# An attention-and-mixing kernel: a searched order for every engine, paired score blocks, longer rows for q and k, weights in halves

## The chip, the cores and the metric

One core of a Trainium2 chip. The metric is device time in microseconds (us) of a whole execution, and lower is better. Fast executions of one kernel differ by up to about 1% (the kernel before: 191.07 to 193.41 us in one set of rounds), so every ratio here is between fast runs made in the same rounds on the same chip. Three runs of the kernel before are slow and left out: 287.37 us (TensorE's granted clock at 0.557), 193.45 and 193.88 us.

In the profile PE is TensorE's matmuls, PEld its weight loads, DVE VectorE, ACT ScalarE, POOL GpSimd and SP the engine that starts transfers. "The span" is the profiled execution without its launch; the time lies about 2 us over it.

## The reference, cut to what matters

```python
def _attn_ref(q, k, v, n_sink, window):          # q, k, v: 4 batches, 8 heads, 768 positions, 64
    scores = scale * np.matmul(q, k.transpose(0, 1, 3, 2))
    keep = is_sink | in_window                    # the first 4 positions, and the last 128
    scores = np.where(keep, scores, -1e9)
    a = softmax(scores)                           # (cut)
    return np.matmul(a, v)

def _moe_ref(x, mu_k, mu_r, w_k, w_v, w_r):       # x: 4 x 768 x 512, the attention's result
    x_prev = ...                                  # x, one position later (cut)
    xk = mu_k * x + (1.0 - mu_k) * x_prev
    xr = mu_r * x + (1.0 - mu_r) * x_prev
    k = np.maximum(xk @ w_k, 0.0)                 # the "hidden layer", 512 -> 1024
    v = k * k @ w_v                               # its "product", 1024 -> 512
    r = 1.0 / (1.0 + np.exp(-(xr @ w_r)))         # the "gate"
    return r * v
```

Of the kernel before, what the change touches and what calls it, by code (L numbers as in the profile page):

```python
# [18 lines left out]


class Plan:

# [8 lines left out]
    def __init__(self):  # L31
        self.ops, self.pools, self.buf = [], {}, {}

# [3 lines left out]
    def op(self, engine, cost, emit, rank, reads=(), writes=(), take=(), hold=(), port=False,  # L37
           lag=None, service=0.0):
        self.ops.append(dict(engine=engine, cost=cost, emit=emit, rank=rank, reads=list(reads),
                             writes=list(writes), take=list(take), hold=list(hold), port=port,  # L40
                             lag=90.0 if lag is None else lag, service=service))

    def schedule(self):
# [21 lines left out]
        owner = {key: pool for o in ops for pool, key in o["take"]}  # L65
        free = {name: [(0.0, j) for j in range(len(t))] for name, t in self.pools.items()}
# [8 lines left out]
        ready = {}  # L75
        for i, o in enumerate(ops):
            at[i] = 0.0
            if not left[i]:
                ready.setdefault(o["engine"], set()).add(i)
        clock, port, dma = {}, {}, 0.0  # L80
# [3 lines left out]
        while len(order) < len(ops):  # L84
            best = None
            for engine, some in ready.items():
                now = clock.get(engine, 0.0)
                pick = None
                for i in some:
                    o = ops[i]  # L90
                    t = max(now, at[i])
                    if o["port"]:
                        t = max(t, port.get("DVE" if engine == "POOL" else "POOL", 0.0))
                    ok = True
                    for name, _ in o["take"]:
                        if not free[name]:
                            ok = False
                            break
                        t = max(t, min(free[name])[0])
                    if not ok:  # L100
                        continue
                    if pick is None or (t, o["rank"], i) < (pick[0], ops[pick[1]]["rank"], pick[1]):
                        pick = (t, i)
                if pick is None:
                    continue
                t0 = pick[0]
                if best is None or t0 < best[0]:
                    best = (t0, pick[1])
# [3 lines left out]
            ready[o["engine"]].discard(i)  # L112
            for name, key in o["take"]:
                b = min(free[name])
                free[name].remove(b)
                where[key] = b[1]
                self.buf[key] = self.pools[name][b[1]]
            clock[o["engine"]] = t + o["cost"]
# [3 lines left out]
            if o["service"]:  # L122
                dma = max(dma, t + o["cost"] + 1300.0) + o["service"]
                end = dma + 600.0
            o["start"], o["end"] = t, end
            order.append(i)
# [5 lines left out]
            for j, whole in then[i]:  # L132
# [8 lines left out]
                if not left[j]:  # L141
                    ready.setdefault(ops[j]["engine"], set()).add(j)
        return order

    def run(self):
        for i in self.schedule():
            self.ops[i]["emit"]()
# [3 lines left out]
def kernel(  # L151
# [34 lines left out]
    pool("sc", 1, [128, 2, 512], FP32, psum)  # L186
    pool("bank", 6, [128, 512], FP32, psum)
    for name in ("ks", "qs", "vs"):
        pool(name, 3, [128, 2, H, D], FP32)
# [39 lines left out]
    def load(u, names, rank, h0=0, h1=H):  # L229
        b, T = divmod(u, NT)  # L230
        for name in names:
            src = {"k": k, "q": q, "v": v}[name]
            for g in range(2):
                s0 = 256 * T + 128 * g

                def emit(key=(name, u), src=src, g=g, s0=s0):
                    nc.sync.dma_start(  # L237
                        out=buf[key][:, g, h0:h1, :],
                        in_=src[b, h0:h1, s0:s0 + 128, :].rearrange("h p d -> p h d"))
                rows = 128 * (h1 - h0)  # L240
                first = g == 0 and h0 == 0
                P.op("SP", rows * 0.9 + 60.0, emit, rank, service=rows * 1.19 + 60.0,
                     take=[(name + "s", (name, u))] if first else (),
                     hold=() if first else [(name, u)],
                     writes=[(name, u, g, hp) for hp in range(h0 // 4, (h1 + 3) // 4)])

    def load_weight(dst, src, key, service, rank):
        P.op("SP", 1000.0, lambda: nc.sync.dma_start(
            out=dst, in_=src.rearrange("(c p) f -> p c f", p=128)), rank, service=service,
            writes=[key])  # L250

    load(0, "kq", -100, 0, 4)
    load(0, "kq", -99, 4, 8)
    load(0, "v", -98)
    load_weight(wk32, moe_w_k, "wk32", 4900.0, -97)
    load(1, "kq", -96)
    load_weight(wr32, moe_w_r, "wr32", 2600.0, -95)
    load(1, "v", -94)
    load_weight(wv32, moe_w_v, "wv32", 5200.0, -93)
    for u in range(2, U):  # L260
        load(u, "kqv", -92 if u == 2 else 10 * u - 18)
# [6 lines left out]
    def const_op(engine, cost, emit, writes=(), reads=(), rank=-50):  # L268
# [3 lines left out]
    const_op("DVE", 300.0, lambda: nc.vector.memset(warm, 0.0), ["warm"])  # L272
    ident32 = tile1([128, 128], FP32, "ident32")
    ident = tile1([128, 128], BF16, "ident")
    const_op("POOL", 500.0, lambda: make_identity(nc, ident32), ["ident32"], rank=-60)
    const_op("POOL", 240.0, lambda: nc.gpsimd.tensor_copy(out=ident, in_=ident32), ["ident"],
             ["ident32"])

    mask = tile1([128, 2, 2, 2, 128], BF16, "mask")
    mask0 = tile1([128, 2, 3, 128], BF16, "mask0")  # L280

    def keep(ap, kind):
        if kind == "U":
            nc.gpsimd.affine_select(out=ap, in_=ap, compare_op=ALU.is_ge, fill=0.0, base=-1,
                                    pattern=[[0, 2], [-1, 128]], channel_multiplier=1)
        else:
            nc.gpsimd.affine_select(out=ap, in_=ap, compare_op=ALU.is_ge, fill=0.0, base=0,
                                    pattern=[[0, 2], [1, 128]], channel_multiplier=-1)

    def make_mask0():  # L290
        nc.gpsimd.memset(mask0, 1.0)
        keep(mask0[:, :, 0, :], "D")
        keep(mask0[:, :, 1, :], "U")
        keep(mask0[:, :, 2, :], "D")
        nc.gpsimd.memset(mask0[0:NS, :, 0:2, :], 1.0)

    def make_mask():
        nc.gpsimd.memset(mask, 1.0)
        for a in range(2):
            keep(mask[:, a, :, 0, :], "U")  # L300
            keep(mask[:, a, :, 1, :], "D")

    const_op("POOL", 2300.0, make_mask0, ["mask0"], rank=-55)

    def make_ones():
        for t in P.pools["vb"]:
            nc.gpsimd.memset(t[:, :, :, D:D + 1], 1.0)

    const_op("POOL", 400.0, make_ones, ["ones"], rank=-54)

    xts = [tile1([128, NC, S + 2], BF16, f"xt{i}") for i in range(2)]

    def make_edges():
        for t in xts:
            nc.gpsimd.memset(t[:, :, 0:2], 0.0)

    const_op("POOL", 200.0, make_edges, ["edges"], rank=-45)
# [3 lines left out]
    hmask = tile1([32, H, D + 1], BF16, "hmask")  # L321

    spread = tile1([128, 128], BF16, "spread")

    def make_spread():
        nc.gpsimd.memset(spread, 0.0)
# [3 lines left out]
    def make_hmask():  # L330
        nc.gpsimd.memset(hmask, 1.0)
        nc.gpsimd.affine_select(out=hmask, in_=hmask, compare_op=ALU.is_ge, fill=0.0, base=0,
                                pattern=[[-4, H], [0, D + 1]], channel_multiplier=1)
        nc.gpsimd.affine_select(out=hmask, in_=hmask, compare_op=ALU.is_ge, fill=0.0, base=3,
                                pattern=[[4, H], [0, D + 1]], channel_multiplier=-1)

    def make_sinks():
        for t in ksink + vsink:
            nc.gpsimd.memset(t, 0.0)
        for t in vsink:  # L340
            nc.gpsimd.tensor_copy(out=t[0:32, :, D:D + 1], in_=hmask[:, :, D:D + 1])

    const_op("POOL", 800.0, make_spread, ["spread"], ["ident"], rank=-44)
    const_op("POOL", 2000.0, make_hmask, ["hmask"], rank=-43)
    const_op("POOL", 2400.0, make_sinks, ["sinks"], ["hmask"], rank=-42)
    const_op("POOL", 2700.0, make_mask, ["mask"], rank=-41)


    wk_sb = tile1([128, NC, Dff], BF16, "wk_sb")
    wr_sb = tile1([128, NC, Dm], BF16, "wr_sb")  # L350
    wv_h = tile1([128, NF, Dm], BF16, "wv_h")
    for i in range(4):
        sl = slice(256 * i, 256 * i + 256)
        P.op("DVE", dve(1024, 0.52), lambda sl=sl: nc.vector.tensor_copy(
            out=wk_sb[:, :, sl], in_=wk32[:, :, sl]), 2 + i, reads=["wk32"], writes=[("wk", i)],
            port=True)
    for i in range(2):
        P.op("DVE", dve(1024, 0.52), lambda i=i: nc.vector.tensor_copy(
# [353 lines left out]
```

## The kernel before: the parts that the change touches

The work is cut into 12 units, each of 256 positions of one batch. The kernel's text lists operations with what they read, write and take from pools of buffers; a planner then puts all of them in one order. It is a greedy planner: at each step it takes the engine that can start soonest, and on it the operation that can start soonest by a small timing model. The order on each engine is then fixed: on the chip an engine never skips an operation whose input is late.

```python
while len(order) < len(ops):
    best = None
    for engine, some in ready.items():
        ...                                       # (cut) earliest start t of each ready operation
                    if pick is None or (t, o["rank"], i) < (pick[0], ops[pick[1]]["rank"], pick[1]):
                        pick = (t, i)
```

Scores use one buffer of two banks of the accumulator memory (PSUM), everything else of TensorE's results the other six banks. The block of scores of one head pair is one operation; it has 64 rows of contraction, and two heads run side by side in the two halves of the array:

```python
pool("sc", 1, [128, 2, 512], FP32, psum)
pool("bank", 6, [128, 512], FP32, psum)
...
for (lhs, o0, o1, rhs) in jobs:
    for a in range(2):
        rows = slice(64 * a, 64 * a + 64)
        nc.tensor.matmul(out=sc[:, a, o0:o1], lhsT=lhs[rows], rhs=rhs[rows], start=True, stop=True)
```

q, k and v are loaded one position and head at a time, 256 bytes each, and each weight in one transfer:

```python
nc.sync.dma_start(out=buf[key][:, g, h0:h1, :],
                  in_=src[b, h0:h1, s0:s0 + 128, :].rearrange("h p d -> p h d"))
...
load_weight(wk32, moe_w_k, "wk32", 4900.0, -97)
```

Eight warm-up matmuls with an operand of zeros run before the first transpose. The masks are stored once per head, and v is cast to 16 bits on GpSimd.

The softmax here doesn't subtract the row's maximum and nothing guards it: scores larger than these inputs give would overflow.

## Time and profile before

| | before |
|---|---|
| time, median of the runs first given (lowest to highest) | 192.47 us (192.15 to 193.44) |
| span of the profiled run (its time) | 189.7 us (191.44) |
| last matmul ends | 186.0 us |
| TensorE streaming in all, from start-to-start distances | 147.9 us |
| of it done by 35.0 us | 12.0 us |
| streaming after 35 us / time that it takes to the last matmul | 135.9 / 151.0 us |

"Streaming" is what the matmuls need when they follow each other without a gap. It has to be worked out from distances between starts, because the busy time in the profile counts the overlap of neighbours twice. The lines that carry this table are in the prediction below; one of the waits from 35 us on is added here. The columns are engine and line, what the wait was for, us in all, times, the longest.

```profile
PEld L476 <- issue: 8.5, 27, 0.7
```

L476 is the score block, and "issue" says that the trace shows no event for which its weight loads waited: this is the time in which TensorE goes into the 64-row form.

### The profile page before, as it was taken

What the parts mean: (1) busy time and instruction counts of PE and PEld (TensorE: products, weight loads), DVE (VectorE), ACT (ScalarE), POOL (GpSimd) and SP (SyncE); (2) the same over time, 40 slices, a digit from 0 to 9 for tenths busy, and PEclk for the clock granted to TensorE, in tenths of its full rate; (3) what the DMA queues carried; (4) which work ended last, traced back from release to release, by engine and by line L of the source; (5) the groups of instructions that cost most, each with busy time, mean ns of one, the idle gap of its engine ahead of it and who ended that gap; (6) DMA issues with size and microseconds to landing.
All of it is one profiled execution on the core that took longest, in us unless ns stands there. A gap on an engine that the chain in (4) does not pass through costs nothing.

```text
span 189.7 us, 4373 instructions
## 1 busy us (share of the span) xinstructions
PE 171.4 (90%) x1676; PEld 111.1 (59%) x1676; DVE 155.9 (82%) x375; ACT 133.4 (70%) x225; POOL 31.9 (17%) x65
## 2 busy tenths in 40 slices
PE   7245699989999999999999999999799999999992
PEld 2123466548647758658549468478368577575740
DVE  0538986999999999989999969989989888888512
ACT  0762767669987978959939859949749679575240
POOL 8990030030420310001501002003400000000000
PEclk9955559999999999999999999999999999999999
DMA  6999989999999999999899891030021030020302
GB/s 109 225 387 252 297 212 358 205 206 225 216 213 276 225 194 252 233 254 235 190 233 278 183 273 59 0 111 3 0 75 41 0 114 0 3 111 0 116 0 111
DMA packets 81573, 30.70 MB, mean 162 GB/s; under 512 B 76432, under 2 KB 76432, under 8 KB 81552
## 3 DMA queue, kind: packets, MB, share of 16 engines
q1 hardware_dynamic: 80496, 30.42, 68.0%
q8 instruction: 13, 0.21, 0.5%
q10 hardware_dynamic: 1056, 0.00, 0.3%
q14 instruction: 8, 0.07, 0.1%
HBM read 24.12 MB, written 6.29 MB: 160 GB/s over the span
## 4 chain that ended last, share of the span: by engine, by line
PE 64%; DVE 20%; DMA 5%; ACT 4%; SPq 4%; issue 2%; ACTq 0%; DVEq 0%
PE bank L598 18%; PE bank L636 18%; PE bank L621 8%; PE sc L476 6%; DMA ks<-in_k_dram 5%; PE bank L517 4%; DVE xk L577 4%; PE bank L395 4%; SPq L237 3%; DVE kk L611 3%; DVE e L493 3%; DVE xr L577 2%; DVE qb L382 2%; PE bank L449 2%; PE bank L556 2%
## 5 line engine op out<-in xcount | busy, mean ns | idle before, releaser
L484 ACT ACTIVATE e<-sc 128x1024 bf16<-128x1024 f32 (+1 forms) x48 | 46.8, 974 | 26.4 <-PE sc L476 26.0
L598 PE MATMUL bank<-xk,wk_sb 128*128 128x256 bf16 x384 | 54.7, 279 | 0.1
L636 PE MATMUL bank<-wv_h,kk 128*128 128x512 bf16 x192 | 47.1, 380 | 0.0
L598 PEld LDWEIGHTS <-wk_sb 128*128 128x128 bf16 x384 | 35.2, 100 | 7.0 <-issue 1.1
L493 DVE TENSOR_TENSOR e<-e,mask 128x1024 bf16<-128x1024 bf16 (+1 forms) x48 | 31.1, 653 | 8.5 <-ACT e L484 8.4
L607 ACT ACTIVATE rl<-bank 128x512 bf16<-128x512 f32 x48 | 29.2, 630 | 7.4 <-PE bank L598 6.6
L413 POOL CAST vb<-vs 128x512 bf16<-128x512 f32 x24 | 17.4, 741 | 74.4 <-DMA vs<-in_v_dram 45.7
L636 PEld LDWEIGHTS <-kk 128*128 128x128 bf16 x192 | 17.1, 98 | 19.1 <-issue 1.1
L621 PE MATMUL bank<-wr_sb,xr 128*128 128x512 bf16 x96 | 24.5, 380 | 0.0
L577 DVE SCALAR_TENSOR_TENSOR xk<-td,mu,xt 128x256 bf16<-128x256 bf16 x48 | 23.2, 507 | 0.5
L611 DVE TENSOR_TENSOR kk<-rl 128x512 bf16<-128x512 bf16 x48 | 21.0, 450 | 2.7 <-ACT rl L607 2.6
L476 PE MATMUL sc<-qt,kt 64*128 64x128 bf16 (+1 forms) x256 | 19.1, 250 | 4.4 <-ACT qt L406 2.6
L577 DVE SCALAR_TENSOR_TENSOR xr<-td,mu,xt 128x256 bf16<-128x256 bf16 x48 | 22.4, 490 | 0.0
L645 DVE SCALAR_TENSOR_TENSOR ob<-th,bank 128x512 f32<-128x512 f32 x24 | 16.3, 681 | 6.7 <-PE bank L636 6.7
L517 PE MATMUL bank<-vb,e 128*128 128x65 bf16 x352 | 20.1, 197 | 1.6 <-DVE e L493 1.5
L517 PEld LDWEIGHTS <-e 128*128 128x128 bf16 x352 | 17.1, 100 | 5.6 <-DVE e L493 2.9
L533 DVE TENSOR_TENSOR x<-bank,rec 128x256 bf16<-128x256 f32 x48 | 19.6, 419 | 0.7
L476 PEld LDWEIGHTS <-kt 64*128 64x128 bf16 x256 | 9.5, 96 | 15.5 <-issue 13.9
L382 ACT CAST kb<-ks 128x512 bf16<-128x512 f32 x24 | 14.9, 667 | 4.6 <-DMA ks<-in_k_dram 4.6
L382 DVE CAST qb<-qs 128x512 bf16<-128x512 f32 x24 | 13.2, 563 | 5.0 <-DMA qs<-in_q_dram 5.0
L406 ACT COPY qt<-bank 128x512 bf16<-128x512 bf16 x24 | 14.9, 622 | 2.9 <-PE bank L395 2.9
L627 ACT ACTIVATE th<-bank 128x512 f32<-128x512 f32 x24 | 15.8, 657 | 1.0 <-PE bank L621 1.0
(49 smaller groups left out, 171.2 us busy)
## 6 DMA issues: line engine op xcount, KB each, us to landing
vs<-in_v_dram SPq DMA_DIRECT2D x24, 256.0 KB, 4.8
out_dram<-ob SPq DMA_DIRECT2D x24, 256.0 KB, 2.2
ks<-in_k_dram SPq DMA_DIRECT2D x22, 256.0 KB, 5.4
qs<-in_q_dram SPq DMA_DIRECT2D x22, 256.0 KB, 5.1
wk<-in_moe_w_k_dram SPq DMA_DIRECT2D x1, 2048.0 KB, 9.3
wv<-in_moe_w_v_dram SPq DMA_DIRECT2D x1, 2048.0 KB, 13.8
wr<-in_moe_w_r_dram SPq DMA_DIRECT2D x1, 1024.0 KB, 7.9
ks<-in_k_dram SPq DMA_DIRECT2D x4, 128.0 KB, 3.4
```

The costliest lines, as they stand in the source:

```text
L382: P.op(by, cost, lambda copy=copy, raw=raw, rk=rk, hs=hs: copy(out=buf[rk][:, :, hs, :], in_=buf[raw][:, :, hs, :]), rank + half, port=by ...
L476: nc.tensor.matmul(out=sc[:, a, o0:o1], lhsT=lhs[rows], rhs=rhs[rows], start=True, stop=True)
L484: nc.scalar.activation(out=buf[ek][:, :, lo:], in_=buf[sck][:, :, lo:], func=AF.Exp, scale=scale)
L493: nc.vector.tensor_tensor(out=buf[ek][:, :, lo:], in0=buf[ek][:, :, lo:], in1=m, op=ALU.mult)
L517: nc.tensor.matmul(out=o[:, g, a, :], lhsT=e[:, a, e0:e0 + 128], rhs=rhs, start=(T == 0 and i == 0), stop=(i == len(blocks) - 1), skip_gro ...
L533: P.op("DVE", dve(256), lambda ok=ok, rk=rk, c=c: nc.vector.tensor_tensor(out=buf["x", u][:, :, 128 * c:128 * c + 128].rearrange("p g (a d ...
L577: nc.vector.scalar_tensor_tensor(out=buf[key][:, c0 + i, :], in0=buf[tk][:, i, :], scalar=mu[w][:, c0 + i:c0 + i + 1], in1=xt[:, c0 + i, t ...
L598: nc.tensor.matmul(out=ps[:, i, :], lhsT=wk_sb[:, c, 128 * f:128 * f + 128], rhs=xk[:, c, :], start=(c == 0), stop=(c == NC - 1), skip_gro ...
L607: P.op("ACT", act(512), lambda psk=psk, rk=rk: nc.scalar.activation(out=buf[rk], in_=buf[psk].rearrange("p (i t) -> p i t", i=2), func=AF. ...
L611: P.op("DVE", dve(512, 0.52), lambda f2=f2, rk=rk: nc.vector.tensor_tensor(out=buf["kk", u][:, 2 * f2:2 * f2 + 2, :], in0=buf[rk], in1=buf ...
L621: nc.tensor.matmul(out=buf[psk], lhsT=buf["xr", u][:, c, 128 * g:128 * g + 128], rhs=wr_sb[:, c, :], start=(c == 0), stop=(c == NC - 1))
L636: nc.tensor.matmul(out=buf[psk], rhs=wv_h[:, f, :], lhsT=buf["kk", u][:, f, 128 * g:128 * g + 128], start=(f == 0), stop=(f == NF - 1))
```

## The change

Its intent is to shorten the loading start and to remove TensorE's gaps after it. Five things change together:

1. The greedy choice is replaced by a fixed list for each engine, found beforehand by swapping operations in the timing model.
2. Score blocks of two head pairs run one after the other as one operation, with two score buffers (four banks), which leaves four banks for all else.
3. q and k are loaded with two neighbouring positions per row, 512 bytes. The transposed copies then hold even and odd positions apart, and ScalarE writes them with a stride when it empties the bank.
4. w_k and w_v come in halves, and loads of other units go between them.
5. Filling matmuls on zeros are put into TensorE's gaps before 45 us of the model, to keep its clock up; set-up work moves from GpSimd to VectorE, and so does the first cast of v.

```diff
+ORDER = {
+    "PE": (
+        77, 80, 93, 83, 86, 104, 96, 119, 101, 107, 125, 129, 122, 112, 116, 145, 136, 91, 171,
...                                              (cut: 324 + 379 + 226 + 32 + 79 places)
-        while len(order) < len(ops):
+        lines = {engine: list(line) for engine, line in ORDER.items()}
+        while any(lines.values()):
...
+                while t - now > 300.0 and now < self.fill_until:
...                                              (cut: takes a free bank)
+                    now += 225.0
+                    order.append(("fill", self.pools["bank"][b[1]]))
...
-    pool("sc", 1, [128, 2, 512], FP32, psum)
-    pool("bank", 6, [128, 512], FP32, psum)
+    pool("sc", TOGETHER, [128, 2, 512], FP32, psum)             # TOGETHER = 2
+    pool("bank", 8 - 2 * TOGETHER, [128, 512], FP32, psum)
...
+                out=buf[key][:, h0:h1, :, :].rearrange("p h j d -> p h (j d)"),
+                in_=src[b, h0:h1, 256 * T:256 * T + 256, :].rearrange(
+                    "h (p j) d -> p h (j d)", j=2)), rank,
...
+LOADS = ("kq0", "v0", "kq1", "wka", "v1", "wkb", "wr", "wva", "wvb")
...
+                    out=buf[key][:, 2 * half:2 * half + 2, :, :].rearrange(
+                        "p c g (t j) -> p c j (g t)", j=2),
...
+                     emit=lambda cs=cs: [scores(i) for i in cs], rank=r, lag=PE_LAG,
+                     take=[("sc", ("sc", u, i)) for i in cs],
```

## The prediction

> **What bounds the kernel now.** I read the page first, then stretches of 5 us, the timeline of TensorE, the counts of matmuls up to the time at which the weights are in, and the waits.
>
> ```profile
> span 189.7 us, 4373 instructions
> PE 171.4 (90%) x1676; PEld 111.1 (59%) x1676; DVE 155.9 (82%) x375; ACT 133.4 (70%) x225; POOL 31.9 (17%) x65
> ...
> PEclk9955559999999999999999999999999999999999
> ...
> PE 64%; DVE 20%; DMA 5%; ACT 4%; SPq 4%; issue 2%; ACTq 0%; DVEq 0%
> ```
>
> TensorE carries most of the chain that ends last, with VectorE next. TensorE's clock is at half in slices 2 to 5.
>
> ```profile
> 5.00:10.00 5.00, 1.56 (x16) 1.04 (x17) 2.81 (x2) 3.66 (x7) 4.86 (x10) 0.88 1.29 230
> 10.00:15.00 5.00, 2.46 (x18) 1.17 (x18) 1.95 (x3) 3.23 (x5) 3.81 (x9) 0.50 1.00 395
> 15.00:20.00 5.00, 2.26 (x32) 1.91 (x31) 4.53 (x12) 1.59 (x4) 0.00 (x0) 0.50 1.27 216
> 20.00:25.00 5.00, 3.65 (x31) 2.64 (x30) 3.89 (x12) 3.65 (x6) 0.00 (x0) 0.50 1.08 301
> 25.00:30.00 5.00, 5.00 (x34) 3.10 (x32) 5.00 (x9) 3.14 (x5) 1.67 (x2) 0.57 0.85 271
> ```
>
> The columns are the stretch, its length, busy time of PE, PEld, DVE, ACT and POOL, the granted clock, the DMA share and GB/s. Until 25 us TensorE is mostly idle, and what it does runs at half clock, while the DMA is full: 395 GB/s when a weight flows, 216 to 230 GB/s when rows of q, k and v of 256 bytes do. So the start is bound by loading, and made worse by the clock.
>
> Busy time overstates the rest, as matmuls overlap. I take the distance from start to start instead:
>
> ```profile
> 111.45 0.28 PE L517 MATMUL bank<-vb,e 128*128 128x65 bf16 x4
> 111.67 0.40 PE L476 MATMUL sc<-qt,kt 64*128 64x256 bf16 x6
> 112.00 0.61 PE L598 MATMUL bank<-xk,wk_sb 128*128 128x256 bf16 x4
> 112.44 0.39 PE L395 MATMUL bank<-ident,kb 128*128 128x128 bf16 x4
> ```
>
> Four 256-column matmuls take 112.44 - 112.00 = 0.44 us, 0.109 each. In the same way 512 columns take 0.216, 128 take 0.056, 65 take 0.029 and 130 take 0.058. With the page's counts: hidden layer 384 x 0.109 = 41.9, its product 192 x 0.216 = 41.5, gate 96 x 0.216 = 20.7, transposes 288 x 0.056 = 16.1, values 352 x 0.029 + 64 x 0.058 = 13.9, sinks 32 x 0.109 = 3.5, spread 0.9, scores about 9.4 if the two 64-row halves run together. That is 147.9 us of streaming; the span has 42 us more. Where are they?
>
> ```profile
> L598 PE MATMUL bank<-xk,wk_sb 128*128 128x256 bf16 x32 | 6.4, 349 | 0.0
> ...
> L476 PE MATMUL sc<-qt,kt 64*128 64x256 bf16 x16 | 2.9, 356 | 3.7 <-ACT qt L406 1.9 <-ACT e L484 1.8
> L517 PE MATMUL bank<-vb,e 128*128 128x65 bf16 x46 | 2.8, 220 | 0.0
> ...
> L621 PE MATMUL bank<-wr_sb,xr 128*128 128x512 bf16 x8 | 2.1, 379 | 0.0
> ```
>
> These are the groups of the first 34.5 us (the last weight is cast from 34.2 on). Weighted as above, all groups in that stretch make 11.3 us of streaming. So 23 us are lost in the first 34.5. From there to the last matmul's end near 186.0, 136.6 us of streaming take 151.5: 15 lost. The tail is 3.7 (last VectorE operation at 186.1, then the store).
>
> ```profile
> ACT e L484 <- PE sc L476: 26.0, 27, 2.1
> ...
> PEld L476 <- issue: 13.9, 37, 1.1
> ```
>
> The second line is the score blocks. In the timeline above the values before them need 4 x 0.029 and end at 111.57; the next full-row matmul starts at 112.00. The block takes 0.43 where three concurrent pairs of 256, 128 and 128 columns need 0.21, so entering and leaving the 64-row form costs about 0.21 us. I count 46 such groups in the instruction order, about 37 after 34.5 us: 7.9 of the 15 us lost. The other 7 are waits, mostly for VectorE:
>
> ```profile
> 132.38 0.48 DVE L577 SCALAR_TENSOR_TENSOR xr<-td,mu,xt 128x256 bf16<-128x256 bf16 x1
> 132.78 1.58 DVE L577 SCALAR_TENSOR_TENSOR xk<-td,mu,xt 128x256 bf16<-128x256 bf16 x2
> ```
>
> Two operations that take 0.40 each from start to start take 1.50 while GpSimd casts v (it is busy 3.73 us between 130 and 135). TensorE then waits over 1 us for a masked score block at 135.
>
> **What the Trainium skill says.**
> "TensorE: Matmul & The Clock Gate", Part 1, has warm matmuls at N/2.4 GHz + 2.5 ns (55.6 and 215.7 ns) and a clock at half after about 3.4 us of idleness. The trace agrees: 56 and 216 ns, and 0.50 after the eight warm-up matmuls ended at 4.9 us.
> "TensorEngine Tiling (Array Packing)", Key Properties, says that a change of tiling mode drains TensorE. The 0.21 us per block agrees.
> "DMA: Bandwidth & Descriptors", Specifications, gives 512 B as the least transfer for line rate. The trace has only one side of it: 256 B at about 216 GB/s, weight rows of 2 to 4 KB at 395.
> "SBUF — State Buffer", two separate sides, says that VectorE and GpSimd lock a port pair against each other. The stretched xk agrees.
>
> **The change part by part.**
> *Scores of two pairs together.* Two score buffers (4 PSUM banks instead of 2), the other pool shrinks from 6 banks to 4. Groups fall from 46 to 24. About 18 of them come after the start: 37 - 18 = 19 fewer x 0.21 = 4.0 us, on the path, since TensorE is the bound there. ScalarE can also do two exponentials without the wait of 26.0 us in the list.
>
> *q and k in rows of 512 bytes.* Per-row estimate from the two rates above: 256 B at 216 GB/s is 1.19 ns, 4096 B at 395 is 10.4 ns, a straight line gives 1.8 ns for 512 B, 285 GB/s. q and k of one unit (256 positions of one batch) are 1.05 MB: 3.7 us instead of 4.9. In return the transposed copies on ScalarE write with a stride; it is busy 70%, so even 0.15 us x 48 hides.
>
> *Order of loads, weights in halves.* With these rates, and the first k at about 4.0 us (4.5 before, less bytes), I add up in the new order: q and k of unit 0 whole at 8, v at 11, k of unit 1 at 13, the first half of w_k at 15.5, q of unit 2 at 18.6, the second half at 21, w_v's first half at 27, w_r at 29.5, the rest of w_v at 34. So the hidden layer of unit 0 can start at about 17 (before: 23.7, at half clock). The last weight is no earlier than before, but more loads of other units have gone ahead of it.
>
> *Filling matmuls.* The eight warm-ups become 42, all ahead of or between the pieces of unit 0's attention: 19 before the first transpose. They should hold the clock at 1.0. Cold ones take 0.43 us, so 19 may end near 7 to 8 us and delay the first transpose by up to 1 us; that is hidden, as w_k is not there before 15.5.
>
> *Sum to 35 us.* In the new order of TensorE I count 12.2 us of streaming ahead of the first product (needs w_v's first half, cast at 27.6), 14.0 ahead of the gate (w_r cast at 31), and 17.6 ahead of the first product that needs the second half of w_v. From 31 on: 17.6 - 14.0 = 3.7 and some switches, so about 35.0 for 17.6 us of work. Before had 11.3 at 34.5: the start gives about 6 us.
>
> *The rest.* 147.9 - 17.6 = 130.3 of streaming, 18 x 0.21 = 3.8 of switches, and other waits, 7 before. The searched order should remove some, four banks may add some: I take 5. That gives 139.1: the last matmul at 174.1, with the tail of 3.7 a span of 177.8. The measured time lies 1.7 to 2.8 us over the span (191.44 in the profiled run and 192.47 median against 189.7), so about 180.
>
> *Moved to VectorE.* Memsets before data comes (hidden) and the cast of the first v, 2 x 0.34. The masks shrink and repeat by a stride of zero; same sizes computed, no change.
>
> **The rivals.**
> *VectorE becomes the bound.* From start to start one unit with a full window needs q casts 2 x 0.335, masks 4 x 0.60, reciprocals and x 4 x 0.43, differences 2 x 0.34, mixes 8 x 0.395, squares 4 x 0.335, outputs 2 x 0.60: 11.2 us, plus up to 1.3 of GpSimd's lock. TensorE needs 12.8 + 0.4. With both over 90% full, every slip of a fixed order shows. For it: VectorE is at 4.9 to 5.0 of 5 us between 40 and 70. Then the waits go to 12 us: time 187.
> *Four banks starve TensorE.* A unit takes 19 banks; in 13.2 us each of four may be held 2.8 us (before, with six, 4.1). Fills of 0.45 to 1.7 us plus 0.6 of evacuation fit, unless an evacuation is late. Worth 0 to 5 us.
> *The start is not better*, because the clock falls anyway where the filling matmuls stop, or 512-byte rows are no faster: the 6 us shrink to 2, time 184.
> *The order beats my guess*: waits of 1 us, time 176.
>
> **Range and chances.** Rivals two to four move the 180 by -4 to +5, and the first by +7. They would hardly all come together, since a slow start leaves slack for VectorE. I put 179.5, 8 in 10 within 174 to 186. Within 2% means over 188.6: it needs the start's gain and the switches' both lost.
>
> **What would show it.** Clock 1.0 from 10 us to the end; DMA near 285 GB/s while q and k flow; the first hidden-layer matmul at 16 to 18 us; 24 score groups, with two blocks in about 0.64 us; the wait of the weight loads of scores down to about half of 13.9; the last matmul near 174. I am wrong if the clock falls again, if TensorE has more than 10 us of waits for banks or for VectorE after 35 us, or if the hidden layer starts after 20 us.

## The result, and the profile after

The changed kernel takes 183.54 us (median of 4 runs, 183.11 to 184.3), the kernel before 192.46 in the same rounds (192.15 to 193.44). The ratio is 0.9532, with a 95% interval of 0.9486 to 0.9579. Ratios here are the mean time of one kernel's fast runs over that of the other's fast runs of the same rounds, so they are not quite the ratio of the medians. The verdict is faster, inside the predicted range and 4.0 us over the predicted time.

From the page, the span, the busy times, the clock and the chain that ended last:

```profile
span 181.3 us, 4366 instructions
...
PE 169.3 (93%) x1687; PEld 114.2 (63%) x1710; DVE 152.9 (84%) x389; ACT 139.0 (77%) x225; POOL 23.2 (13%) x47
...
PEclk9999759999999999999999999999999999999999
...
PE 73%; DVE 19%; ACT 4%; issue 2%; DVEq 0%
```

TensorE now carries 73% of the chain (before 64%), and no transfer is in it any more. The clock falls later and for a shorter time than before, but it does fall. (1710 weight loads and 1687 matmuls: 23 matmul records are missing, each of which looks like a gap of up to 0.22 us in the timeline.)

The stretches from 15 us on, with the same columns as in the prediction:

```profile
15.00:20.00 5.00, 2.81 (x45) 1.98 (x43) 3.13 (x10) 4.07 (x8) 0.61 (x1) 1.00 1.13 310
20.00:25.00 5.00, 3.47 (x27) 2.04 (x29) 4.24 (x12) 3.33 (x5) 0.71 (x1) 0.50 1.07 285
25.00:30.00 5.00, 4.91 (x58) 3.99 (x59) 4.89 (x11) 4.16 (x8) 0.48 (x1) 0.82 1.01 355
30.00:35.00 5.00, 4.25 (x64) 3.30 (x61) 4.94 (x14) 4.12 (x9) 0.00 (x0) 1.00 1.10 354
```

Loading is faster between 15 and 20 us (310 GB/s in place of 216), yet TensorE has little more to do than before. And from 25 us on VectorE, the third busy column, is full (TensorE's busy time, the first, counts overlap twice). The timeline of unit 0 says why (start, length, engine, line, what; in brackets the idle time before and what ended it):

```profile
4.01 0.62 ACT L507 CAST kb<-ks 128x512 bf16<-128x512 f32 x1 [1.41 <-DMA ks<-in_k_dram]
5.82 0.43 DVE L507 CAST qb<-qs 128x512 bf16<-128x512 f32 x1 [1.91 <-DMA qs<-in_q_dram]
7.86 0.39 PE L519 MATMUL bank<-ident,kb 128*128 128x128 bf16 x4
...
18.01 0.59 ACT L704 COPY xt<-bank 128x512 bf16<-128x512 bf16 x1 [0.46 <-PE bank L698]
...
19.20 0.66 DVE L484 CAST wk_sb<-wk 128x1024 bf16<-128x1024 f32 x1
20.11 0.68 DVE L484 CAST wk_sb<-wk 128x1024 bf16<-128x1024 f32 x1
21.05 0.42 DVE L709 TENSOR_TENSOR td<-xt 128x512 bf16<-128x512 bf16 x1
...
24.92 0.83 DVE L719 SCALAR_TENSOR_TENSOR xk<-td,mu,xt 128x256 bf16<-128x256 bf16 x1
26.30 1.29 PE L740 MATMUL bank<-xk,wk_sb 128*128 128x256 bf16 x8
33.25 0.68 DVE L482 TENSOR_SCALAR wv_h<-wv 128x1024 bf16<-128x1024 f32 x1
35.33 1.03 PE L778 MATMUL bank<-wv_h,kk 128*128 128x512 bf16 x4
```

The first half of w_k landed at 16.9 us, but the first hidden-layer matmul runs at 26.30, later than before (23.7). It waits for xk, the last piece of which VectorE finishes at 24.92 + 0.83 = 25.75. VectorE could have started the difference for it when the copy of x ended at 18.60; in its order the casts of w_k and pieces of other work come first, and it starts at 21.05. That is the first half of x. The last xk needs the second half, which is copied only at 22.69, and then two casts of q and one xr stand before and between the pieces of xk. TensorE puts four transposes ahead of the hidden layer after that. In the same way the first half of w_v landed at 28.5 and is cast only from 33.25 to 35.2; the first product follows at 35.33. The prediction had counted 12.2 us of streaming ahead of this product and put it at 27.6: the work ahead of it was right, and it came 7.7 us later.

The trace of before shows the same wait. There w_k had landed at 16.2 us (6.92 + 9.3), and the hidden layer started at 23.74, when xk was ready.

Counting the matmuls of the first 35.0 us and giving each its start-to-start distance, the changed kernel has 12.2 us of streaming done (hidden layer 32 x 0.109, values 56 x 0.029, their sinks 8 x 0.058, scores 20 x 0.109 / 2 and 32 x 0.056 / 2, transposes 64 x 0.056, sinks 8 x 0.109, spread 0.2), the kernel before 12.0 in the same way (it has fewer transposes, and eight gate matmuls). So the whole expected head start shrinks to 0.2 us.

Then the score blocks, in TensorE's timeline at the place that the prediction showed of before:

```profile
112.47 1.04 PE L740 MATMUL bank<-xk,wk_sb 128*128 128x256 bf16 x8
113.44 0.61 PE L602 MATMUL sc<-qt,kt 64*128 64x256 bf16 x12
113.98 0.40 PE L698 MATMUL bank<-ident,x 128*128 128x128 bf16 x4
```

Eight hidden-layer matmuls take 8 x 0.109 and end their streaming at 113.34. The next full-row matmul starts at 113.98: 0.64 us for two blocks that need 2 x 0.22 (0.109 + 2 x 0.056 each), so one switch costs 0.20 for two blocks, where at the place shown of before it was 0.21 for each. Taking this difference at every switch after 35 us that no wait interrupts gives 0.200 to 0.211 us for 38 of the 40 before and 0.201 to 0.205 for 18 of the 19 after, in the middle 0.202 both times. The corresponding wait from 35 us on:

```profile
PEld L602 <- issue: 1.3, 6, 0.3
```

The 8.5 us of before have become 1.3. Here is the whole account, with a switch taken as 0.202 us:

| | before | after | gain |
|---|---|---|---|
| streaming done by 35.0 us | 12.0 | 12.2 | 0.2 |
| last matmul ends | 186.0 | 177.6 | |
| time from 35 us to there | 151.0 | 142.6 | |
| streaming in that time | 135.9 | 135.7 | (the 0.2 above) |
| lost in that time | 15.1 | 6.9 | |
| of it switches | 40 x 0.202 = 8.08 | 19 x 0.202 = 3.84 | 4.24 |
| other waits | 7.02 | 3.06 | 3.96 |
| tail after the last matmul | 3.7 | 3.7 | 0 |

0.2 + 4.24 + 3.96 = 8.4 us, which is 189.7 - 181.3. The third experiment measures the price of a switch in another way. (The total of 147.9 us is the prediction's. From the same distances the scores need 9.7 us, not 9.4, which takes 0.3 us from the other waits on both sides and leaves the gain.)

Loading, from the page's line of packets:

```profile
DMA packets 57124, 30.69 MB, mean 169 GB/s; under 512 B 26896, under 2 KB 51472, under 8 KB 57104
```

Before, 76432 of 81573 packets were under 512 B; now 26896 of 57124 are, and 24576 of these are rows of v.

### The profile page after: what moved, and what is told of

The parts are those of the page before. It is cut to its first block, busy times and chain, and to the rows that moved or that the text cites. A ratio compares the mean times of both kernels' runs of the same rounds, so it can differ in the third digit from the quotient of the medians.

```text
span 181.3 us, 4366 instructions
## 1 busy us (share of the span) xinstructions
PE 169.3 (93%) x1687; PEld 114.2 (63%) x1710; DVE 152.9 (84%) x389; ACT 139.0 (77%) x225; POOL 23.2 (13%) x47
## 2 busy tenths in 40 slices
DMA packets 57124, 30.69 MB, mean 169 GB/s; under 512 B 26896, under 2 KB 51472, under 8 KB 57104
## 4 chain that ended last, share of the span: by engine, by line
PE 73%; DVE 19%; ACT 4%; issue 2%; DVEq 0%
PE bank L778 20%; PE bank L740 18%; PE bank L763 10%; PE sc L602 6%; PE bank L798 5%; PE bank L659 5%; PE bank L519 5%; DVE xk L719 3%; PE bank L698 3%; DVE xr L719 3%; DVE e L636 2%; DVE x L675 2%; PE bank L647 2%; DVE kk L753 2%; ACT e L622 2%
## 5 line engine op out<-in xcount | busy, mean ns | idle before, releaser
L740 PE MATMUL bank<-xk,wk_sb 128*128 128x256 bf16 x384 | 51.9, 274 | 0.7 <-ACT th L769 0.4
L622 ACT ACTIVATE e<-sc 128x1024 bf16<-128x1024 f32 (+1 forms) x48 | 44.8, 963 | 1.0 <-PE sc L602 0.9
L749 ACT ACTIVATE rl<-bank 128x512 bf16<-128x512 f32 x48 | 27.9, 608 | 13.5 <-PE bank L740 6.5
L763 PE MATMUL bank<-wr_sb,xr 128*128 128x512 bf16 x87 | 23.7, 379 | 0.5
L719 DVE SCALAR_TENSOR_TENSOR xr<-td,mu,xt 128x256 bf16<-128x256 bf16 x48 | 23.3, 497 | 0.1
L527 ACT COPY qt<-bank 128x512 bf16<-128x512 bf16 x24 | 17.9, 744 | 7.0 <-PE bank L519 6.9
L753 DVE TENSOR_TENSOR kk<-rl 128x512 bf16<-128x512 bf16 x48 | 19.8, 425 | 1.5 <-ACT rl L749 1.5
L527 ACT COPY kt<-bank 128x512 bf16<-128x512 bf16 x24 | 17.8, 743 | 2.6 <-PE bank L519 2.6
L704 ACT COPY xt<-bank 128x512 bf16<-128x512 bf16 x24 | 14.1, 587 | 6.4 <-PE bank L698 6.2
L769 ACT ACTIVATE th<-bank 128x512 f32<-128x512 f32 x24 | 14.1, 606 | 4.0 <-PE bank L763 4.0
L602 PE MATMUL sc<-qt,kt 64*128 64x128 bf16 (+1 forms) x256 | 14.7, 248 | 0.9 <-ACT kt L527 0.8
```

The source lines that it names most:

```text
L527: nc.scalar.copy(out=buf[key][:, 2 * half:2 * half + 2, :, :].rearrange("p c g (t j) -> p c j (g t)", j=2), in_=buf[psk].bitcast(BF16)[:, ...
L622: nc.scalar.activation(out=buf[ek][:, :, lo:], in_=buf[sck][:, :, lo:], func=AF.Exp, scale=scale)
L719: nc.vector.scalar_tensor_tensor(out=buf[key][:, c0 + i, :], in0=buf[tk][:, i, :], scalar=mu[w][:, c0 + i:c0 + i + 1], in1=xt[:, c0 + i, t ...
L740: nc.tensor.matmul(out=ps[:, i, :], lhsT=wk_sb[:, c, 128 * f:128 * f + 128], rhs=xk[:, c, :], start=(c == 0), stop=(c == NC - 1), skip_gro ...
L749: P.op("ACT", act(512), lambda psk=psk, rk=rk: nc.scalar.activation(out=buf[rk], in_=buf[psk].rearrange("p (i t) -> p i t", i=2), func=AF. ...
L753: P.op("DVE", dve(512, 0.52), lambda f2=f2, rk=rk: nc.vector.tensor_tensor(out=buf["kk", u][:, 2 * f2:2 * f2 + 2, :], in0=buf[rk], in1=buf ...
```

## The experiments

The theory after this reading: TensorE sets the end after the start; fewer switches and fewer waits brought the gain, and the waits went because the searched order hides what four banks would otherwise cost. The start brought nothing because a fixed order holds unit 0 back on VectorE and ScalarE. The rivals: the gain comes from the start's loads; it comes from pairing alone, whatever the order; VectorE is the bound; the half clock or the filling matmuls at the start eat a gain that would be there. The texts were written for each run before it; letters in them are names for the theories that they describe.

Times are medians of 6 runs. Every kernel was timed in five rounds, and differences in us against the changed kernel are the difference of the two ratios times 192.46. The changed kernel was not timed again in these rounds, which ran on four chips; each ratio's interval is about 1 us to either side, so a difference under about 1.4 us is not clear of noise.

### The searched order undone, all else changed

```diff
-        lines = {engine: list(line) for engine, line in ORDER.items()}
-        while any(lines.values()):
+        waiting = set(range(len(ops)))
+        while waiting:
...
-                if ok and (best is None or t < best[0]):
+                if ok and (best is None or (t, o["rank"], i) < (best[0], ops[best[1]]["rank"], best[1])):
```

> The changed kernel with the searched order undone: the same operations, buffers, costs and filling matmuls, but each engine takes the operation that its timing model says can start first, as the kernel before did. Theory A (after 35 us the searched order removed about 2.5 to 3 us of TensorE's waits, beside the 4.5 us of score switches): 2 to 5 us slower than the changed kernel's 183.5, 185.5 to 188.5. Rival B (the order is worth nothing, pairing and loads give all of the 8.9 us): 183 to 184.5. Rival C (with four banks the greedy order starves TensorE and the order was needed to make pairing pay at all): over 190.

196.55 us, ratio 1.0224 (1.0175 to 1.0272): slower than the kernel before, though whether by 2% is left unclear. This is what rival C expected; theory A fell 8 us short. All other parts of the change together lose without the order. The trace shows where: its start is the best of all runs (hidden layer at 21.5 us, 15.7 us of streaming by 35 us, the clock at full until 56.3), but from 35 us on it needs 156.9 us for 132.2 of streaming. With 20 x 0.202 = 4.0 of switches, about 21 us are lost otherwise. Their causes were not told apart; waits are not all of it, as the clock is at half from 56.3 to 59.7 and from 179.2 to 186.0. The order of the loads is undone too, but the first half of w_k lands at 16.3 us, nearly as in the changed kernel. So an earlier start can be had with these loads, and it did not decide the end.

### q and k in rows of 256 bytes again

```diff
-                out=buf[key][:, h0:h1, :, :].rearrange("p h j d -> p h (j d)"),
+                out=buf[key][:, h0:h1, j, :],                   # for j in range(2)
...
-                    "h (p j) d -> p h (j d)", j=2)), rank,
+                    "h (p j) d -> p h j d", j=2)[:, :, j, :]) for j in range(2)], rank,
```

> The changed kernel with q and k loaded in rows of 256 bytes again (two transfers for each, even and odd positions; layout, order and all else as changed). If loading still binds the start (first 35 us) by its bandwidth, q and k of units 0 to 2 (3.1 MB, 3.7 us longer at 216 instead of 285 GB/s) arrive later and the time grows by 2 to 4 us, to 185.5 to 187.5. If the start is bound by the chain through VectorE, ScalarE and the half clock instead, which the trace suggests (the hidden layer of unit 0 starts at 26.3 us although its weights have landed at 16.9 us), under 1.5 us: 183.5 to 185.

186.8 us, ratio 0.9714 (0.9655 to 0.9773), 3.5 us over the changed kernel. By 35 us it has 11.1 us of streaming in place of 12.2, less than the kernel before, and the hidden layer starts at 27.0. So the searched order needs the longer rows not to fall behind at the start. The run changes the rows and with them the number of transfers, so the 3.5 us belong to both.

### A switch put back between the two blocks of a pair

```diff
+            if switch:                                          # ahead of the second block of a pair
+                nc.tensor.matmul(out=sc[:, 0, 128:256], lhsT=warm[:, 0:128], rhs=warm[:, 0:128],
+                                 start=True, stop=True)
```

> The changed kernel with one small matmul of full-row form (128 columns, its result overwritten) between the two score blocks of each pair: 24 more changes of the form, as many as before, at 0.056 us of own work. Theory (each change in and out costs 0.21 us and TensorE sets the end after 35 us): 19 of the 24 come after 35 us, 19 x 0.27 = 5.1 us, so 187.5 to 189. Rival (VectorE sets the end, TensorE has slack): under 1.5 us more, 183.5 to 185.

189.7 us, ratio 0.9855 (0.9802 to 0.9908), 6.2 us over the changed kernel. TensorE's timeline:

```profile
112.95 0.40 PE L605 MATMUL sc<-qt,kt 64*128 64x256 bf16 x6
113.28 0.23 PE L596 MATMUL sc<-warm 128*128 128x128 bf16 x1
113.44 0.40 PE L605 MATMUL sc<-qt,kt 64*128 64x256 bf16 x6
113.77 1.05 PE L743 MATMUL bank<-xk,wk_sb 128*128 128x256 bf16 x8
```

Two blocks now take 113.77 - 112.95 = 0.82 us against 0.54 from start to start in the changed kernel: 0.28 for each inserted matmul, of which 0.056 is its own streaming. All 24 pairs together would make 24 x 0.28 = 6.7; 6.2 are seen. A little work in TensorE's way comes out of the end almost one for one, so TensorE sets the end here, and the price of a switch is about 0.2 us by this measurement too (6.2 / 24 - 0.056). The 6.2 us are over the 5.1 expected, which counted only the pairs after 35 us; by 35 us this trace has 11.1 us of streaming, 1.1 less than the changed kernel's.

### Fewer filling matmuls ahead of the first transpose (11 for 19)

```diff
-                    now += 225.0
+                    now += 430.0 if now < 3600.0 else 225.0
```

> The changed kernel with 11 instead of 19 filling matmuls ahead of the first transpose (the cold ones counted at 0.43 us). In the changed kernel's trace k was cast at 4.63 us and q at 6.25, but the transposes came at 7.86 and 8.73 because the 19 fill until 7.9. Theory (this delay runs down the chain of unit 0's attention and holds up the hidden layer): the first transposes come at 6.3 to 6.7 us, the hidden layer of unit 0 about 2 us earlier, time 1 to 2 us less: 181.5 to 182.5. Rival (the delay is absorbed, as my prediction said): no change, 183 to 184.

182.37 us, ratio 0.9484 (0.9435 to 0.9532), 0.9 us less, with intervals that overlap. The first transpose runs at 5.4 us instead of 7.86, but the hidden layer only 0.7 us sooner, at 25.6 (this trace is of the longest of the six runs, 184.25 us). The 2.4 us that the cold fills cost at the head of unit 0's chain are mostly taken up again behind it, and whether anything is left is not clear of noise.

### Sixteen more filling matmuls, in unit 0's gaps

```diff
+EXTRA = {107: 4, 145: 4, 171: 6, 156: 2}
...
+                for _ in range(EXTRA.get(i, 0)):                # ahead of operation i, into its own bank
+                    name, key = self.ops[i]["take"][0]
+                    self.fill(self.buf[key][:, 0, :] if name == "sc" else self.buf[key])
```

> The changed kernel with 16 more filling matmuls at four places where TensorE waited between 15 and 23 us (4 ahead of the third value block, 4 and 2 ahead of unit 1's score pairs, 6 ahead of unit 2's first q transposes). In the changed kernel the clock falls to half from 20.0 to 26.8 us, in which about 3.5 us of streaming are done. Theory A (the half clock lengthens the chain to the hidden layer): the clock stays at 1.0, unit 0's hidden layer starts 1 to 2 us earlier, time 1 to 2.5 us less, 181 to 182.5. Rival B (in this stretch the chain runs through VectorE and ScalarE, and the clock does not matter): the clock stays up and the time stays within 0.7 us of 183.5. If the clock falls all the same, this run does not tell.

182.59 us, ratio 0.9527 (0.9472 to 0.9582), the same as the changed kernel. The clock did stay up from end to end:

```profile
PEclk9999999999999999999999999999999999999999
```

So the half clock at 20 to 27 us costs nothing that shows in the time. Theory A was right about the chain, though: unit 0's hidden layer starts at 24.7, 1.6 us earlier, and by 35 us 13.3 us of streaming are done, 1.1 more. Of this 0.5 us is left when the last matmul ends (177.1), too little to show in the time. So the half clock is a part of the lost start, but not of the lost time, and a lead at 35 us need not last to the end.

### Less work for VectorE

```diff
-            P.op("DVE", dve(width, 0.52), masked, r, ...
+            P.op("DVE", dve(width, 0.52), masked if not T or c < 2 else masked_less, r, ...
```

The mask of half the head pairs covers a quarter of the block, 6.4 us less of VectorE in all; the result is wrong (relative error 0.118).

> Wrong on purpose: in the 8 units with a full window, half of the mask multiplications cover 256 instead of 1024 elements, so VectorE loses 16 x about 0.4 = 6.4 us of work and all else stays. If TensorE sets the end after 35 us (as the switch test says), under 1.5 us less, 182 to 183.5. If VectorE sets it, 4 to 6 us less, 177.5 to 179.5.

183.28 us, ratio 0.9556 (0.9507 to 0.9605): no change. VectorE is not what sets the end by itself.

### Less work for TensorE

```diff
+                n = 2 if 2 <= u <= 10 else NC
-                for c in range(NC):
+                for c in range(n):
```

Half of the gate's products are left out in nine units: 9 x 2 x 2 x 0.216 = 7.8 us less. (The output still lay within the comparison's tolerance, but it is not the right sum.)

> Wrong on purpose: the gate of units 2 to 10 sums two instead of four blocks, so TensorE loses 18 x 2 x 0.216 = 7.8 us of streaming and all else stays. If TensorE alone sets the end after 35 us, 6.5 to 7.8 us less, 175.5 to 177. If VectorE is nearly as full (its work from start to start is about 139 us), it takes over and only 2 to 5 us come out, 178.5 to 181.5.

180.88 us, ratio 0.9436 (0.9382 to 0.9489): only 1.8 us less. Most of what was taken away comes back as waits. From 35 us on, its matmuls wait longest for VectorE, where no matmul of the changed kernel waited over 0.4:

```profile
PE bank L779 <- DVE kk L753: 1.1, 1, 1.1
PE bank L647 <- DVE x L675: 0.9, 2, 0.5
```

L779 is the product, which reads kk. L647, the values of the sinks, does not read x: it waits for a bank that VectorE empties late. These lines are 2.0 of the 6 us; the rest was not told apart.

### Both at once (wrong on purpose)

The edits of the last two runs together.

> Wrong on purpose: both reliefs at once, 6.4 us of mask work less on VectorE and 7.8 us of gate matmuls less on TensorE. Alone the first gave nothing (ratio 0.956 against 0.953) and the second 1.9 us. Theory (after 35 us TensorE is the bound and VectorE is close behind): together clearly more than the sum, 4 to 6.5 us less than 183.5. Rival (the fixed order with four banks is the bound, whichever engine is relieved): about the sum, 1.5 to 2.5 us less.

179.5 us, ratio 0.9332 (0.9287 to 0.9377): 3.8 us less than the changed kernel, where the two alone gave +0.5 and -1.8. They help each other by 2.5 us, of which noise could make about 2, so VectorE is close behind TensorE. But 3.8 of 7.8 us is under what was expected of the pair, so something besides these two holds it as well. The fixed order is one candidate, as it was searched for the full load; the run does not show it.

### Weights whole again

```diff
+        whole = ({"wk": wk32, "wv": wv32}[name], ...) if part else (dst, src)
-        P.op("SP", 1000.0, lambda: nc.sync.dma_start(out=dst, in_=src), rank, service=service,
+        P.op("SP", 1000.0, (lambda: None) if part == "b" else
+             lambda: nc.sync.dma_start(out=whole[0], in_=whole[1]), rank, service=service,
```

> The changed kernel with w_k and w_v loaded whole again, each in the place of its first half (the second half's place is empty); order and casts as changed. If halving helps the start, because other loads pass between the halves: 1 to 3 us slower, 184.5 to 186.5. If it does not matter or its shorter rows cost what it gains (w_k's halves have rows of 2 KB and landed at about 320 GB/s, the whole before at 374): within 0.7 us of 183.5.

184.79 us, ratio 0.9646 (0.9596 to 0.9696), 2.2 us more. The halves are worth something in this order. The whole weight takes the place of the first half, and delays the loads that followed that half.

### The kernel before, with pairing alone

```diff
-    pool("sc", 1, [128, 2, 512], FP32, psum)
-    pool("bank", 6, [128, 512], FP32, psum)
+    pool("sc", 2, [128, 2, 512], FP32, psum)
+    pool("bank", 4, [128, 512], FP32, psum)
...
+            if c % 2 == 0:
+                P.op("PE", 640.0 if T else 500.0, lambda ...: [scores(c), scores(c + 1)], r,
```

> The kernel before with the pairing alone: two score buffers, four banks, the scores of two head pairs as one operation (cost 0.64 and 0.50 us in its timing model), its own greedy choice of order, rows of 256 bytes, whole weights, eight warm-up matmuls. If pairing pays by itself, 22 fewer changes of form x 0.21 = 4.6 us less than before, ratio 0.976. If with four banks a greedy order loses more in waits than the switches give, as the greedy run of the changed kernel (196.6 us) suggests, at or above before: ratio 1.00 to 1.03.

193.4 us, ratio 1.0054 (1.0002 to 1.0105): no gain at all, although 24 groups took the place of 46. From 35 us on its trace has 153.7 us for 136.2 of streaming, 17.5 lost. Switches are 20 x 0.202 = 4.0 (before 8.1), the other waits 13.5 (before 7.0). The saving was spent again, and the waits of its matmuls in that stretch name a part of what spent it (the last line is VectorE's timeline):

```profile
PE bank L640 <- DVE x L537: 2.9, 1, 2.9
PE bank L396 <- DVE x L537: 0.8, 4, 0.3
PE bank L509 <- ACT rl L611: 0.7, 1, 0.7
34.14 2.50 DVE L364 TENSOR_SCALAR wv_h<-wv 128x1024 bf16<-128x1024 f32 x4 [1.00 <-DMA wv<-in_moe_w_v_dram]
```

The line and the releaser have to be read together. L640 is the product, L396 the transposes of q and k, L509 the scores of the sinks: none of these reads what the releaser makes (x, or the hidden layer's rl), so at the end of the wait it is the bank which that operation empties that is missing. The longest is not all the bank's: TensorE waits from 34.3 to 37.2 us for its first product, which needs w_v as well, and the second of w_v's four casts ends at 35.4. So at most 1.8 of the 2.9 us are the bank's, and together 1.8 + 0.8 + 0.7 = 3.3 us of the 6.5 by which the waits grew. In the kernel before no such wait in that stretch is over 0.3 us. This run settles most of the theory: pairing pays nothing under the greedy order, and with the first run, which had everything but the searched order, it shows that pairing and order pay together. That the banks eat up to 3.3 of the 4.1 us which the switches saved is read from these lines; no run gave the greedy order more banks, and none had a searched order without pairing.

### Contiguous evacuation

```diff
-                    out=buf[key][:, 2 * half:2 * half + 2, :, :].rearrange(
-                        "p c g (t j) -> p c j (g t)", j=2),
+                    out=buf[key][:, 2 * half:2 * half + 2, :, :],
```

The positions end up in the wrong places (the output lay within the tolerance all the same). This tests what the stride costs. The group of q's copies in the changed kernel:

```profile
L527 ACT COPY qt<-bank 128x512 bf16<-128x512 bf16 x24 | 17.9, 744 | 7.0 <-PE bank L519 6.9
```

744 ns against 622 before.

> Wrong on purpose: ScalarE writes the transposed q and k side by side again instead of with a stride of two elements (positions come out in another order). In the changed kernel these 48 copies take 0.74 us instead of 0.60 of before, and 0.59 instead of 0.475 from start to start: 5.5 us of ScalarE. If that is hidden, as predicted: 183 to 184. If ScalarE, 77% busy, holds others up: 1 to 3 us less.

183.39 us, ratio 0.9533 (0.9492 to 0.9575): the same. The strided copies are hidden, as predicted.

### The order searched again, with cold fills priced

The fills' cost of the fourth run, and lists found by more swaps from the given ones; about a quarter of the places differ (73 of 324 on TensorE, 117 of 379 on VectorE).

```diff
-        77, 80, 93, 83, 86, 104, 96, 119, 101, ...
+        (other lists for PE, DVE, ACT, POOL and SP; cut)
```

> A try at a better version, not a test of one part: the changed kernel with its cold filling matmuls counted at 0.43 us in its own timing model (10 instead of 19 ahead of the first transpose) and its order searched further with single moves in that model (about a quarter of the places differ, most of them in the start). The model's own gain is 0.6 us. If the start's chain is what is left to win, as the run with fewer filling matmuls hints (ratio 0.948 against 0.953): 181 to 182.8. If the order is at its limit and the chip does not follow the model to half a microsecond: 183 to 185.

181.4 us (181.12 to 182.16), ratio 0.9421 (0.9379 to 0.9463). This beats both kernels: its interval lies below that of the changed kernel. It overlaps that of the run with fewer fills (0.9435 to 0.9532), whose edit it contains, so what the new order adds by itself is not clear of noise. By 35 us it has 13.8 us of streaming, and its last matmul ends at 176.75. The hidden layer starts at 25.2 us, sooner than in the changed kernel, although the first half of w_k now lands 5.2 us later (22.1 for 16.9), as the list of the loads was searched as well:

```profile
25.18 0.61 PE L750 MATMUL bank<-xk,wk_sb 128*128 128x256 bf16 x4 [0.39 <-DVE wk_sb L494]
```

Here TensorE waits for the cast of w_k, and xk is ready by 21.3. So part of the head start that the prediction saw can be had by the order, the loads' among it, with transfers of the same size.

## Why the prediction was right or wrong

**The start: the step that failed.** "The start gives about 6 us" became 0.2: 12.2 us of streaming by 35 us in place of 17.6. Two terms of that step can be checked apart. The loads were nearly right: 512-byte rows of q flowed at 524 KB in 1.85 us, 283 GB/s, against 285, and the landings came only 1 to 3 us late (first half of w_k 16.9 for 15.5, of w_v 28.5 for 27). What failed is the sentence that "the hidden layer of unit 0 can start at about 17". I let TensorE go on as soon as a weight had landed, and counted what stood ahead of it in TensorE's own order. I did not follow the chain of unit 0 through the fixed orders of VectorE and ScalarE, nor the cast of w_v, which I put at 27.6 and which was done at 35.2. There the last xk was done at 25.75 and the cast of w_v ran 4.75 us after its landing. It could have been read from the trace of before, where the hidden layer started 7.5 us after w_k had landed. The greedy run (21.5 us, with w_k landing at 16.3) shows that w_k's landing was not the limit, and that run and the searched-again one (15.7 and 13.8 us by 35 us) that the order decides a part of it. The half clock is another part (1.1 us of streaming in the run with a full clock). No run came near 17 or 17.6; what else holds unit 0 was not separated.

The prediction named three signs of being wrong, and two came true: the clock fell, and the hidden layer started after 20 us. Its rival "the start is not better" had the time (184) and the falling clock, but rows of 512 bytes were faster. That 183.54 us still lies within 174 to 186 is partly luck: the waits were 2 us better than guessed, and the range was wide enough for the rest.

**The filling matmuls: hidden, but not as told.** I expected up to 1 us of delay for the first transpose, hidden behind the load of w_k. It was about 2.4 us, since 19 fills ran until 7.86 although k and q were cast by 6.25. Since xk and not the weight came last, w_k could not hide it; what hid most of it was slack further down the chain, because fewer fills brought only about 0.9 us, which is not clear of noise. That they "should hold the clock at 1.0" was wrong: the clock fell at 20.0 us, and not after 3.4 us of idleness. TensorE was busy for 2.07 of the 3.40 us before, with no gap over 0.86. In before it fell at 8.8, with no gap over 1.7 since the warm-ups, so the prediction's "the trace agrees" was too quick. It did not matter for the time, as the run with a full clock shows.

**The switches: right.** 4.0 us were predicted (37 groups to 18 or 19 at 0.21), 4.2 found (40 to 19 at 0.202). The time of two blocks, "about 0.64 us", was met exactly. The run with a switch put back gives 6.2 us for 24 of them.

**The other waits: better than the guess.** I took 5 us, "7 before"; found were 3.1 and 7.0. The rival "the order beats my guess" is the one that came true, and it made good part of the start's loss. The rival of four banks is true as well, but of another kernel: under the greedy planner with pairing alone the other waits grew by 6.5 us, up to 3.3 of them seen as waits for banks, and under the searched order no matmul's wait in that stretch is over 0.4 us.

**The hidden costs: right.** Strided copies did not show. No run tested the moved set-up work by itself; it ended before the first q, for which VectorE then waited 1.91 us. **VectorE as the bound: not yet.** It is full in most stretches up to 70 us, and taking work from it alone changes nothing; taking work from TensorE alone brings a quarter of it.

**The sum.** The last matmul was predicted at 174.1 and came at 177.6, 3.5 us later: 5.4 less streaming by 35 us, the same switches (3.8), 1.9 less of other waits (3.1 for 5), and 5.4 - 1.9 = 3.5. The tail of 3.7 was right. Of the remaining 0.5 us to the 4.0, 0.4 are the median over the profiled run (183.54 and 183.11).

**What stays open.** How much of the 4.0 us of saved waits is due to each engine's list was not split, and a searched order without pairing, with six banks, was not built. The cast of v on GpSimd, which stretched xk in the trace of before, was not tested by itself (one xk of 0.83 us at 24.92 looks like it again).

## What to carry to other kernels

A start-up estimate must follow the first unit's data through every engine's fixed order up to the matmul in question; when a load lands is only the earliest that its user could run. Saving time on the engine that sets the end pays only if the buffers given up for it do not bring the waits back, so try such a trade together with the order, and look at the waits for buffers after it. Before repairing something that looks bad in a profile, such as a half clock or a slower copy, take it away once and see whether the time moves.

## What the Trainium skill lacked or had wrong

- "TensorE: Matmul & The Clock Gate", Part 1, has in its table the half clock after an idle window of about 3.4 us. Here it fell at 20.0 us although TensorE had no gap over 0.86 us in the 3.4 us before. (Further down it has short idle times as another cause, without a size.) The page also does not say how to tell whether the half clock costs time: a kernel with the clock up throughout took the same time as one with it at half for 7 us (ratios 0.9527 and 0.9532), though its hidden layer started 1.6 us earlier. The kernel before, in ten fast runs on one chip, showed a mean clock of either 0.945 to 0.947 or 1.0, with mean spans of 190.8 and 190.2 us.
- "TensorEngine Tiling (Array Packing)", Key Properties, names the drain at a change of tiling mode and gives no size. Here it was 0.20 us (0.200 to 0.211 at 56 places) for going into the 64-row form and out again, and 24 more of them made the kernel 6.2 us slower.
- "DMA: Bandwidth & Descriptors", Specifications, has 512 B as the least for line rate. Here 512-byte rows flowed at 283 GB/s (7.5 to 9.0 us of the changed kernel) and weight rows of 2 KB at 405 (25.0 to 26.5 us), so 512 B was better than 256 B (about 216) but not the full rate.
- No page that I read treats engines that are nearly full together in a fixed order: 7.8 us less for TensorE brought 1.8, 6.4 less for VectorE nothing, both 3.8.
